# Exponential pieces in single buffers, some of them made by an accumulating DMA, with a new set of planner limits

## The chip, the cores and the metric

The kernel runs on one core of a Trainium2 chip. The metric is the device time of one execution in microseconds. The core has a tensor engine (TensorE; PE in the profile, with its weight loads as PEld), a vector engine (VectorE, DVE), a scalar engine (ScalarE, ACT), GpSimd (POOL), a sync engine that issues DMAs (SyncE, SP), and 16 DMA engines.

## The reference

Two attention blocks over one input are mixed by a gate. Only the first, the full attention, is touched by the change in its inner part.

```python
x = A_x                                            # 1 x 2048 x 512, 32 heads of 16
g = _sigmoid((x * gate_w).sum(-1, keepdims=True))
# A: full attention
scores = jnp.einsum("bhqd,bhkd->bhqk", q, k) * Dh ** -0.5
p = _softmax(scores, axis=-1)
a = (p @ v) @ wo
# B: each query sees 8 keys, at distances 0, 2, .. 14
logits = jnp.einsum("bhsd,bhswd->bhsw", q, kg) * Dh ** -0.5
b = (_softmax(masked logits) @ vg) @ wo
return g * a + (1 - g) * b
```

The 32 heads x 2048 queries x 2048 keys of A make 134 million exponentials, and they are most of the work.

## The kernel before

**Tiles.** A score tile is 128 keys by 512 queries of one head. There are 2048: 32 blocks (four column groups `ct`, four query chunks `qc`, two parities `par`), and in each 16 key tiles `kt` for four heads `j`. A tile is made by one matmul with 32 rows (L1870; four heads stand in four row groups of the array), or, for key tile 9, by four column-tiled matmuls on a spread copy of the keys (`kz`, L1855). Its exponential is multiplied with the values (`vaug`, which carries a column of ones for the denominator) by a matmul with 128 rows and 32 columns (L1643), four of them side by side in the array, one for each head.

**Two ways to an exponential.** ScalarE takes two or three tiles out of PSUM in one instruction (L1924) and writes bf16 to one of eight `pt` tiles. VectorE takes single tiles of the key tiles in `KD` (L1562): one multiply and add that ends as an int16, whose bits are read as an fp16, which is a coarse power of two. One such piece is too coarse, so the exponential is the sum of `NP_` = 3 pieces, whose bits differ by a constant, with three weights. Pieces 1 and 2 are made from piece 0 by adding a constant (`piece`: L1571 on VectorE, or L1569 on POOL, which adds pairs of int16 as one int32). The weights sit in scaled copies of the values (`vaugw`), so each such tile costs three product matmuls in place of one. Up to four tiles (`YB_ITEMS`) form a batch, whose pieces are made by one instruction of up to 128 x 2048.

**Buffers.** A batch holds one of three `yb` buffers, each with room for all three pieces (3 x 2048 int16 to a partition). It comes free when all of its product matmuls are out (`ref["refs"]` in `emit_pv_one`).

**The order.** The order on each engine is written out by a planner (`run`) when the kernel is built. It keeps a clock for each engine, always moves the one that is furthest behind, and picks its next work by due times, readiness and limits (`tune`). TensorE refills one of two PSUM slots with scores for ScalarE (three banks and two) when the slot is free; otherwise it does product matmuls, or a step of the other work (projections, the whole of attention B, output projections). `d_wanted` says whether VectorE is to take a tile too; it asks that a buffer is free and that VectorE's backlog is under a limit. `LEVELS` holds the possible values of each limit and `STRETCH` which of them holds in each of 64 equal stretches of the program. `TUNE` holds the release and due times of the other work. Each engine then runs its list in order; what it waits for are semaphores.

**POOL and VectorE.** A POOL step is made to wait for the last VectorE instruction marked `port` that stands before it (in `take_step`), and the planner does not start a marked VectorE step while POOL is busy by its clock.

**The end.** `outproj_last` handles the last two output tiles. Their two casts (L1472, one on VectorE and one on ScalarE) fill the halves of one tile, and the last of them issues one DMA for both (L1475).

Of the kernel before, what the change touches and what calls it, by code (L numbers as in the profile page):

```python
# [40 lines left out]
PW_S = tuple(s - math.log2(3.127444) for s in (0.0, -0.3330078125, 0.3330078125))  # L41
NP_ = len(PW_S)
KD = (2, 4, 7, 9, 12, 14)
KZ = (9,)
# [3 lines left out]
NPT = (4, 4)  # L48
NYB = 3
NQM = 3  # L50
# [4 lines left out]

TUNE = dict(relL=64, dueL2=2040, R0=74, R1w=42, R1g=20, R2g=31, R3g=46, R3w=50, dueB=61, dueL=84, v2rel=79, v2step=21, v2due=91, krel=230, krel2=192, ahead=0.142, dueV=30, dueS=115, dueO=678, dlast=62, qrel=28, prelB=59, prodrel=-12)

LEVELS = dict(
    pool=(0.0, 0.4, 1.2, 2.5, 4.0),
    backlog=(0.758, 1.231, 1.61, 1.894, 2.273, 2.841, 3.788),  # L60
    backlog_s=(0.888, 1.442, 1.886, 2.219, 2.663, 3.329, 4.438),
    part_us=(0.6, 0.975, 1.275, 1.5, 1.8, 2.25, 3.0),
    misc_slack=(-32, -18, -12, -8, -4, 2, 16),
    urgent=(-25, -11, -5, -1, 3, 9, 23),
    fit=(0.0, 0.2, 0.3, 0.4, 0.5, 0.6, 0.8),
    port=(0.338, 0.549, 0.718, 0.845, 1.014, 1.268, 1.69),
    alone=(-8.973, -0.273, -0.123, 0.027, 0.177, 0.327, 9.027),
    grab=(1, 0, 2, 3, 4),
    lend=(1, 0, 2, 3, 4, 5, 6, 7),
    order=((-1, 0, 1, 2, 1), (-1, 1, 0, 2, 3), (-1, 0, 2, 1, 3), (-1, 0, 1, 2, 3), (1, 0, 1, 2, 3), (0, 0, 1, 2, 3), (1, 0, 2, 1, 3), (2, 0, 1, 2, 3)),  # L70
)
STRETCH = dict(
    pool="1343344333433432333333333333232333333333333330333301233333333333",
    backlog="3333333333133333333333333333633333663333433463333133346332333333",
    backlog_s="3330413333333333333333323333033331333333631333333333331333332333",
    part_us="6333115334333333333333333533333333333643633330333335333333363303",
    misc_slack="3336333333533323333333333333333333333033333323333333433333303333",
    urgent="3341331533633333332533333333333333333333333303333333230333033331",
    fit="3613335633413353333333330333333111333333333340323333031333133333",
    port="3333533433333333333333332333333333435333333333333333333533333333",  # L80
    alone="2333333333333303333323333313333335133533303333333333333333333333",
    grab="0004204000034000030000003000000000000300000040000000300000000300",
    lend="0001000200000010000000000600000000000000000000401000006000020000",
    order="3003600020460000000144002001060007000000600020000000500060072000",
)
# [636 lines left out]
T_P1 = lambda n: n / 390.0 + 0.2  # L722
T_PI = lambda n: n / 1150.0 + 0.12
T_P2 = lambda n: n / 470.0 + 0.065
MM = 0.216
# [29 lines left out]
class _Fast:  # L755
# [15 lines left out]
    def setup(self):  # L771
# [17 lines left out]
                   for a, (w, n) in enumerate(zip(ACT_W, NPT))]  # L789
        self.yb = [c([P, NP_, YB_ITEMS * 512], I16, name=f"yb{i}") for i in range(NYB)]  # L790
        self.oT = [c([P, S], BF16, name=f"oT{i}") for i in range(2)]
# [76 lines left out]
        nc.gpsimd.memset(self.halo[:], 0.0)  # L868
        for k in range(1, NP_):
            nc.gpsimd.memset(self.pc[:, k:k + 1], round(1024.0 * (PW_S[k] - PW_S[0])) * 65537)  # L870
        self.idx = pidx, pf, ei, ef
# [587 lines left out]
    def outproj_last(self, st, i, norm):  # L1459

        nc = self.nc

        def mmh(srcs):
            for br, ct in srcs:
                o = self.oT[ct] if br == "A" else self.oB(ct)
                w = self.woA if br == "A" else self.woB
                self.mm4(self.misc, lambda c: o[:, st * 128 + 32 * c:st * 128 + 32 * c + 32], w[:, ct, :],
                         start=(br == "B" and ct == 0), stop=(br == "A" and ct == 3))

        def ev():  # L1470
            ob = self.eg[:].bitcast(BF16).rearrange("p (t n) -> p t n", t=2)
            (nc.scalar.copy if i else nc.vector.tensor_copy)(out=ob[:, i, :], in_=self.misc[:])  # L1472
            self.out_left -= 1
            if self.out_left == 0:
                nc.sync.dma_start(out=self.o_dst[:, st - i:st - i + 2, :], in_=ob)  # L1475
        order = [("B", c) for c in range(4)] + [("A", c) for c in range(4)]
        ch = self.chain([("PE", 2 * MM, lambda: mmh(order[0:2])), ("PE", 2 * MM, lambda: mmh(order[2:4])),
                         ("PE", 3 * MM, lambda: mmh(order[4:7])), ("PE", MM, lambda: mmh(order[7:])),
                         (("DVE", "ACT")[i % 2], T_D1(512), ev)],
                        due=TUNE["dueL2"] + i, rel=2048 - TUNE["relL"], deps=[self.oB_done[(st // 4, c)] for c in range(4)])  # L1480
        ch[3].deps.append(norm)
        for s in ch[:4]:
            s.hold = False

    def run(self):
        self.out_left = 2
        nc, tc = self.nc, self.tc
# [16 lines left out]
        pt_refs = {}  # L1504
        yb_free = [0.0] * NYB
        batch = None
# [52 lines left out]
        def exp_dve(slot_item):  # L1559
            (b, kt, j), bt, i, bank = slot_item  # L1560
            A = SCALE * math.log2(math.e) * 1024.0
            return nc.vector.tensor_scalar(out=self.yb[bt["buf"]][:, 0, i * 512:(i + 1) * 512], in0=bank[:],  # L1562
                                           scalar1=A, scalar2=1024.0 * (15.0 + PW_S[0]), op0=ALU.mult, op1=ALU.add)

        def piece(bt, k, gp=False):
            n = len(bt["items"]) * 512
            y = self.yb[bt["buf"]]
            if gp:
                return nc.gpsimd.tensor_tensor(out=y[:, k, 0:n].bitcast(I32), in0=y[:, 0, 0:n].bitcast(I32),  # L1569
                                               in1=self.pc[:, k:k + 1].to_broadcast([P, n // 2]), op=ALU.add)  # L1570
            return nc.vector.tensor_scalar(out=y[:, k, 0:n], in0=y[:, 0, 0:n],  # L1571
                                    scalar1=float(round(1024.0 * (PW_S[k] - PW_S[0]))), scalar2=None, op0=ALU.add)

        def close_batch():
# [3 lines left out]
            n = len(bt["items"]) * 512  # L1578
            bt["refs"] = NP_ * len(bt["items"])
            parts = [dict(n=NP_) for _ in bt["items"]]  # L1580

            def done(k, end):
                for i, it in enumerate(bt["items"]):
                    add_pv(it, self.yb[bt["buf"]][:, k, i * 512:(i + 1) * 512].bitcast(F16), end, ("y", bt, k), parts[i])
            now = min(t.values())
            pl = max(0.0, t["POOL"] - now) + sum(s.cost for s in self.steps if s.eng == "POOL" and s.rel <= p
                                                 and ready_time(s) <= now + 1.0)
            for k in range(1, NP_):
                gp = pl < tune("pool") and n >= 1024
                pl += gp * T_PI(n)  # L1590
                s = Step("POOL" if gp else "DVE", T_PI(n) if gp else T_D4(n), lambda k=k, gp=gp: piece(bt, k, gp),
                         deps=list(bt["p1"]), due=bt["due"], cls=2)
                s.on_done = lambda end, k=k: done(k, end)
                s.port = not gp
                self.steps.append(s)
            last = bt["p1"][-1]

            def after(end, prev=last.on_done):
                prev(end)
                done(0, end)  # L1600
            if last.end is None:
                last.on_done = after
            else:
                done(0, last.end)

# [8 lines left out]
        def emit_pv_one(j, now):  # L1614
# [17 lines left out]
            else:  # L1632
                ref["refs"] -= 1
                if ref["refs"] == 0:
                    yb_free[ref["buf"]] = now + 0.45
            out = self.flex[acc[b]][32 * j:32 * j + 32, :]
# [131 lines left out]
        def d_wanted(now, flex=True):  # L1768

            if p >= N - 8 or p % 64 >= TUNE["dlast"] or not any(k in KD for r in rem[p // 64] for k in r):  # L1770
                return False
            if batch is None and min(yb_free) > now:
                return False
# [36 lines left out]
        def d_add(it, bank, p1done):  # L1810
# [3 lines left out]
            if batch is None:  # L1814
                buf = min(range(NYB), key=lambda i: yb_free[i])
                batch = dict(buf=buf, items=[], p1=[], due=0.0, blk=b)
                yb_free[buf] = INF
            bt = batch
# [66 lines left out]
        while True:  # L1885
# [80 lines left out]
            else:  # L1966
# [27 lines left out]
                else:  # L1994
# [21 lines left out]
                    full = len(av) == 4  # L2016
                    part = av and (free_p <= 1 or min(yb_free) > now + 0.5 or cold(now) or now - old > tune("part_us") or (cur == NB - 1 and left[cur] <= len({(e[1], j) for j, q in enumerate(pvq) for e in q})) or p >= N)
                    pick = None
# [93 lines left out]
```

## Time and profile before

| | us |
|---|---|
| time, median of 3 runs (703.13 to 704.62) | 703.66 |
| the profiled execution: its time | 703.66 |
| its span, first to last instruction | 701.8 |
| last exponential of ScalarE ends | 692.3 |
| last DMA is issued | 696.4 |

The profile's engine shares count the time in which an engine had at least one instruction under way. TensorE's matmuls overlap, so a busy TensorE may still do more. The chain of waits gives 55% of the span to TensorE, 21% to ScalarE and 9% to VectorE. The granted clock of TensorE was 0.997 of full speed. The DMA engines are little used in the first half of the program (slices of 0 to 2 tenths after the start) and 3 to 6 tenths busy in the second, when attention B spreads its weights and values.

A line of the groups reads: source line, engine, operation, what it writes and reads, shapes, count; then busy us and mean ns of one; then the engine's idle time just before them and what ended it. A line of the DMA issues ends with the KB of one and the median us from issue to landing.

### The profile page before, as it was taken

Reading aid. Unit: us, or ns where it says so; the run is one execution under the profiler, and the core shown is the slowest. Engines: PE = TensorE matmul, PEld = TensorE weight load, DVE = VectorE, ACT = ScalarE, POOL = GpSimd, SP = SyncE. Lnnn points to the kernel's source line nnn. Section 1 sums busy time; section 2 is a strip of 40 time slices with the busy share of each in tenths; the row PEclk is TensorE's granted clock in tenths of the full one; section 3 lists DMA queues with packets and bytes.
Section 4 is the critical chain, followed back from the end, with each engine's and each line's share of the span. In section 5 each row is a group of like instructions: output and inputs, shape, how many; then the busy total and the mean of one; then the engine's idle time right before and its main releaser. Section 6 shows DMA issues by size and latency. Waiting matters only on the chain.

```text
span 701.8 us, 21325 instructions
## 1 busy us (share of the span) xinstructions
PE 679.5 (97%) x8556; PEld 218.2 (31%) x8556; DVE 651.8 (93%) x1093; ACT 680.6 (97%) x696; POOL 429.3 (61%) x364
## 2 busy tenths in 40 slices
PE   9999999999999999999998999999999999999996
PEld 4432222233322232223332223322233232222343
DVE  6999999997899999999999999999999999989982
ACT  6999999999999999999999999999999999999994
POOL 4766877766476455555456566666557564676671
PEclk9999999999999999999999999999999999999999
DMA  6001101000100100000103236356453644566521
GB/s 174 5 16 36 44 3 31 2 2 9 35 2 16 25 1 5 6 2 9 34 2 92 102 90 157 105 147 157 111 143 95 155 133 107 142 161 167 149 68 35
DMA packets 64473, 48.70 MB, mean 69 GB/s; under 512 B 22512, under 2 KB 63984, under 8 KB 64240
## 3 DMA queue, kind: packets, MB, share of 16 engines
q1 hardware_dynamic: 63808, 45.96, 25.6%
q8 instruction: 69, 1.13, 0.7%
q0 software_dynamic: 288, 1.05, 0.5%
q14 instruction: 36, 0.29, 0.1%
q10 hardware_dynamic: 272, 0.26, 0.1%
HBM read 39.85 MB, written 5.26 MB: 64 GB/s over the span
## 4 chain that ended last, share of the span: by engine, by line
PE 55%; ACT 21%; DVE 9%; issue 6%; SPq 4%; DMA 3%; POOL 1%; DVEq 0%; ACTq 0%; POOLq 0%
ACT pt L1924 21%; PE fps L1870 19%; PE fps L1643 18%; PE fps L895 14%; DVE yb L1562 5%; DVE yb L1571 2%; SPq L1328 1%; DVE prod L1229 1%; SPq L962 1%; PE fps L1855 1%; PE fps L1378 1%; DMA vw<-v_dram 1%; DMA erb<-er_dram 1%; SPq L1354 1%; DMA er<-er_dram 1%
## 5 line engine op out<-in xcount | busy, mean ns | idle before, releaser
L1924 ACT ACTIVATE pt<-fps 128x1024 bf16<-128x1024 f32 (+1 forms) x682 | 674.6, 1141 | 7.7 <-PE fps L1870 5.5
L1562 DVE TENSOR_SCALAR yb<-fps 128x512 int16<-128x512 f32 x584 | 377.0, 678 | 18.2 <-PE fps L1870 15.4
L1870 PE MATMUL fps<-qm,kT 32*128 32x512 bf16 x1976 | 285.9, 384 | 12.7 <-ACT pt L1924 7.8
L1643 PE MATMUL fps<-pt,vaug 128*32 128x512 bf16 (+1 forms) x1562 | 234.7, 372 | 0.4 <-DVE yb L1562 0.4
L1569 POOL TENSOR_TENSOR yb<-yb,pc 128x1024 int32<-128x1024 int32 (+1 forms) x104 | 188.5, 1823 | 64.5 <-DVE yb L1571 15.2
L1643 PE MATMUL fps<-yb,vaugw 128*32 128x512 f16 (+1 forms) x1228 | 174.4, 374 | 0.6 <-POOL yb L1569 0.4
L1870 PEld LDWEIGHTS <-kT 32*128 32x128 bf16 x1976 | 80.9, 91 | 272.1 <-issue 267.2
L1571 DVE TENSOR_SCALAR yb<-yb 128x2048 int16<-128x2048 int16 (+3 forms) x206 | 132.1, 666 | 0.6
L1643 PE MATMUL fps<-yb,vaug 128*32 128x512 f16 (+1 forms) x614 | 113.0, 375 | 0.0
L1360 POOL TENSOR_TENSOR er<-er,vw 128x512 bf16<-128x512 bf16 x64 | 72.8, 1158 | 49.6 <-DVE yb L1571 29.0
L895 PE MATMUL fps<-xT,ww 128*32 128x512 bf16 (+2 forms) x1296 | 99.9, 381 | 0.2
L1360 POOL TENSOR_TENSOR erb<-erb,vw 128x512 bf16<-128x512 bf16 x64 | 72.5, 1156 | 38.4 <-DVE yb L1571 23.2
L1643 PEld LDWEIGHTS <-vaug 128*32 128x32 bf16 x2176 | 64.8, 94 | 81.7 <-issue 74.9
L1643 PEld LDWEIGHTS <-vaugw 128*32 128x32 bf16 x1228 | 45.1, 94 | 41.7 <-issue 35.1
L1229 POOL TENSOR_TENSOR prod<-bq,bk 128x512 bf16<-128x512 bf16 x32 | 34.4, 1076 | 31.4 <-DVE yb L1571 17.4
L895 PEld LDWEIGHTS <-ww 128*32 128x32 bf16 x1296 | 25.9, 95 | 31.7 <-issue 24.0
L1676 POOL TENSOR_TENSOR t<-t,rc 128x512 bf16<-128x512 f32 x15 | 15.9, 1058 | 27.0 <-DVE yb L1571 13.4
L930 POOL TENSOR_SCALAR vaugw<-vaug 128x128 bf16<-128x128 bf16 (+1 forms) x24 | 20.4, 853 | 18.4 <-DVE vaug L923 10.7
L1855 PE MATMUL fps<-qm,kz 128*32 128x512 bf16 x288 | 30.8, 383 | 0.6 <-DVE yb L1562 0.4
L1229 DVE TENSOR_TENSOR prod<-bq,bk 128x2048 bf16<-128x2048 bf16 x24 | 29.9, 1268 | 0.2
L1666 DVE STREAM_TRANSPOSE t<-fps 128x512 f32<-128x512 f32 x32 | 22.6, 706 | 2.3 <-PE fps L1643 1.9
L895 PE MATMUL fps<-woB,oB 128*32 128x512 bf16 x256 | 19.9, 382 | 0.0
(117 smaller groups left out, 306.5 us busy)
## 6 DMA issues: line engine op xcount, KB each, us to landing
vw<-v_dram SPq DMA_DIRECT2D x128, 128.0 KB, 3.1
er<-er_dram SPq DMA_DIRECT2D x128, 64.0 KB, 3.0
erb<-er_dram SPq DMA_DIRECT2D x128, 64.0 KB, 2.9
v_dram<-vs SPq DMA_DIRECT2D x16, 128.0 KB, 2.6
qm<-qs SPq DMA_DIRECT2D x112, 16.0 KB, 1.8
x_in<-in_A_x_dram SPq DMA_DIRECT2D x3, 512.0 KB, 5.4
ww<-in_B_wqkv_dram SPq DMA_DIRECT2D x12, 128.0 KB, 2.8
out_dram<-ob SPq DMA_DIRECT2D x12, 128.0 KB, 2.7
```

What stands on the lines that cost most here:

```text
L895: self.nc.tensor.matmul(out=out_ps[32 * c:32 * c + 32, 0:n], lhsT=lhsT_of(c), rhs=rhs, start=start, stop=stop, tile_position=(0, 32 * c))
L930: return self.nc.gpsimd.tensor_scalar(out=self.vw4[k][:, KD.index(st), h0:h1, 0:DH], in0=self.vaug4[:, st, h0:h1, 0:DH], scalar1=PW_W[k], ...
L1229: return e.tensor_tensor(out=pr[m % 2][:, a:b], in0=bq[ct][:, a:b], in1=bk[ct][:, o + a:o + b], op=ALU.mult)
L1360: return nc.gpsimd.tensor_tensor(out=st_["erb"][m % 4][:, g, :], in0=st_["erb"][m % 4][:, g, :], in1=st_["vw"][m % 2][:, g, :], op=ALU.mult)
L1562: return nc.vector.tensor_scalar(out=self.yb[bt["buf"]][:, 0, i * 512:(i + 1) * 512], in0=bank[:], scalar1=A, scalar2=1024.0 * (15.0 + PW_ ...
L1569: return nc.gpsimd.tensor_tensor(out=y[:, k, 0:n].bitcast(I32), in0=y[:, 0, 0:n].bitcast(I32), in1=self.pc[:, k:k + 1].to_broadcast([P, n ...
L1571: return nc.vector.tensor_scalar(out=y[:, k, 0:n], in0=y[:, 0, 0:n], scalar1=float(round(1024.0 * (PW_S[k] - PW_S[0]))), scalar2=None, op0 ...
L1643: nc.tensor.matmul(out=out, lhsT=v, rhs=r, start=start, stop=stop, tile_position=(0, 32 * j))
L1666: nc.vector.transpose(out=self.t1[:, par].rearrange("p a b -> p (a b)"), in_=self.flex[acc[b]])
L1855: nc.tensor.matmul(out=dst[32 * c:32 * c + 32, :], lhsT=self.kz[:, j, KZ.index(kt), 32 * c:32 * c + 32], rhs=self.qm[(4 * ct + qc) % NQM][ ...
L1870: nc.tensor.matmul(out=dst, lhsT=self.kT[ct % 2][32 * j:32 * j + 32, kt * 128:(kt + 1) * 128], rhs=self.qm[(4 * ct + qc) % NQM][par][32 * ...
L1924: nc.scalar.activation(out=self.pt[pi[0]][pi[1]][:, 0:n * 512], in_=self.aslot[si][:, 0:n, :].rearrange("p a b -> p (a b)"), func=ACT.Exp, ...
```

## The change

- **Single buffers.** Eight slices `ys` (2048 int16 to a partition each) and one constant tile `step` replace the three `yb` buffers; the room is the same. A batch takes one slice for its first piece, and other slices only for the pieces that are made fresh. Each slice is counted down and freed on its own (`slice_dec`). `d_wanted` asks for two free slices.
- **The first piece** is now number 1, and the constants are differences from it: `STEP_OF[0]` and `STEP_OF[2]`, the second twice the first.
- **In place.** When a batch closes, its place in its block of 64 tiles (`pos`) is compared with two limits (`acc1`, `acc2`). Past both, pieces 2 and 0 are made fresh as before; past one, only piece 2; before both, neither. A piece that is not made fresh is made later in the first slice itself: once all readers of what is there are out, POOL issues a DMA that adds the `step` tile to the slice, element by element. This can happen twice, for piece 0 and then for piece 2.
- **Other limits.** `TUNE`, `LEVELS` and `STRETCH` have new values, among them `lend`, whose usual value is now 4: ScalarE's wider slot lends its third bank whenever no other bank is free. The release of the last output projections moves from 64 tiles before the end (`relL`) to 20.
- **The end.** The last two output tiles leave in two DMAs of 128 KB, the first issued by SP and the second by ScalarE, in place of one of 256 KB by SP.

```diff
+STEP_OF = {k: round(1024.0 * (PW_S[k] - PW_S[1])) for k in (0, 2)}
+assert STEP_OF[2] == 2 * STEP_OF[0]
-NYB = 3
+NSL = 8
...
-TUNE = dict(relL=64, dueL2=2040, R0=74, R1w=42, R1g=20, R2g=31, R3g=46, R3w=50, dueB=61, dueL=84, v2rel=79, v2step=21, v2due=91, krel=230, krel2=192, ahead=0.142, dueV=30, dueS=115, dueO=678, dlast=62, qrel=28, prelB=59, prodrel=-12)
+TUNE = dict(relL=20, dueL2=2040, R0=110, R1w=42, R1g=12, R2g=31, R3g=43, R3w=50, dueB=61, dueL=84, v2rel=79, v2step=21, v2due=91, krel=230, krel2=214, ahead=0.142, dueV=-9, dueS=100, dueO=665, dlast=62, qrel=32, prelB=27, prodrel=-12)
...
-        self.yb = [c([P, NP_, YB_ITEMS * 512], I16, name=f"yb{i}") for i in range(NYB)]
+        self.ys = [c([P, YB_ITEMS * 512], I16, name=f"ys{i}") for i in range(NSL)]
+        self.step = c([P, YB_ITEMS * 512], I16, name="step")
...
+        nc.gpsimd.memset(self.step[:].bitcast(I32), STEP_OF[0] * 65537)
...
-            ob = self.eg[:].bitcast(BF16).rearrange("p (t n) -> p t n", t=2)
-            (nc.scalar.copy if i else nc.vector.tensor_copy)(out=ob[:, i, :], in_=self.misc[:])
-            self.out_left -= 1
-            if self.out_left == 0:
-                nc.sync.dma_start(out=self.o_dst[:, st - i:st - i + 2, :], in_=ob)
+            if i % 2 == 0:
+                ob = self.wk.tile([P, D], BF16, name="ob", tag="ob")
+                nc.vector.tensor_copy(out=ob[:], in_=self.misc[:])
+                nc.sync.dma_start(out=self.o_dst[:, st, :], in_=ob[:])
+            else:
+                ob = self.eg[:].bitcast(BF16)[:, 512 * (i // 2):512 * (i // 2) + 512]
+                nc.scalar.copy(out=ob, in_=self.misc[:])
+                nc.scalar.dma_start(out=self.o_dst[:, st, :], in_=ob)
...
+        def slice_dec(bt, sl, at):
+            bt["cnt"][sl] -= 1
+            bt["at"] = max(bt["at"], at)
+            if bt["cnt"][sl]:
+                return
+            if sl != bt["buf"] or not bt["ip"]:
+                ys_free[sl] = bt["at"] if sl == bt["buf"] else at
+                return
+            k = bt["ip"].pop(0)
+            bt["cnt"][sl] = len(bt["items"])
+            n = len(bt["items"]) * 512
+            d0 = Step("X", 0, None)
+            d0.end = bt["at"]
+
+            def acc():
+                nonlocal acc_q
+                acc_q = max(acc_q, t["POOL"] + T_AI) + T_AQ * n / 2048
+                s.lat = acc_q + (T_AL if p < ACC_B else T_ALB) - t["POOL"] - T_AI
+                return nc.gpsimd.dma_start(out=self.ys[sl][:, 0:n], in_=self.step[:, 0:n], accum_op=ALU.add)
+            s = Step("POOL", T_AI, acc, deps=[d0], due=bt["due"], cls=2)
+            s.on_done = lambda end: bt["done"](k, sl, end)
+            self.steps.append(s)
...
+            sls = sorted((i for i in range(NSL) if ys_free[i] <= now), key=lambda i: ys_free[i])[:NP_ - 1]
+            want = (pos >= tune("acc1")) + (pos >= tune("acc2"))
+            fresh = [2, 0][:min(len(sls), want)]
+            bt["ip"] = [k for k in (0, 2) if k not in fresh]
...
-            if batch is None and min(yb_free) > now:
+            if batch is None and sum(x <= now for x in ys_free) < 2:
```

In the built program the instruction counts change so: VectorE's exponentials of single tiles from 584 to 590, its pieces from 206 to 153, POOL's pieces from 104 to 65, accumulating DMAs from none to 90, ScalarE's exponentials from 682 to 702.

## The prediction

> **What bounds the kernel now.** I read the busy shares first, then the groups by shape, then a stretch of TensorE's timeline, then the busy times by stage, the DMA issues and the last microseconds. The shares say that three engines are nearly full and POOL is not.
>
> ```profile
> PE 679.5 (97%) x8556; PEld 218.2 (31%) x8556; DVE 651.8 (93%) x1093; ACT 680.6 (97%) x696; POOL 429.3 (61%) x364
> ```
>
> So no single engine can be relieved for a large gain: ACT's own work is what the rest is fitted around. The groups by shape give the price of each kind of work (busy us, mean ns of one, then idle time before it).
>
> ```profile
> L1924 ACT ACTIVATE pt<-fps 128x1024 bf16<-128x1024 f32 x582 | 555.5, 1078 | 4.8 <-PE fps L1870 3.1 <-PE fps L1643 0.7 <-ACT pt L1924 0.2
> L1562 DVE TENSOR_SCALAR yb<-fps 128x512 int16<-128x512 f32 x584 | 377.0, 678 | 18.2 <-PE fps L1870 15.4 <-PE fps L1855 0.5 <-issue 0.2
> ...
> L1569 POOL TENSOR_TENSOR yb<-yb,pc 128x1024 int32<-128x1024 int32 x94 | 176.9, 1893 | 59.4 <-DVE yb L1571 13.9 <-DVE yb L1562 13.5 <-PE fps L1870 10.2
> ...
> L1924 ACT ACTIVATE pt<-fps 128x1536 bf16<-128x1536 f32 x100 | 150.8, 1508 | 3.0 <-PE fps L1870 2.4 <-ACT pt L1924 0.3
> L1571 DVE TENSOR_SCALAR yb<-yb 128x2048 int16<-128x2048 int16 x178 | 121.4, 704 | 0.5
> ```
>
> An ACT exponential of two tiles lasts 1078 ns and one of three 1508 ns, but back to back they start 0.904 and 1.331 us after one another, since each overlaps its forerunner by 0.17 us. The eight that are merged in the last fence below check it: 4 x 0.904 + 4 x 1.331 + 0.17 = 9.11 against 9.14.
>
> TensorE's price is in its starts, not in its busy time (matmuls overlap). The columns are start, length, instruction, count:
>
> ```profile
> 100.36 0.39 PE L1870 MATMUL fps<-qm,kT 32*128 32x512 bf16 x2
> 100.68 0.61 PE L895 MATMUL fps<-xT,ww 128*32 128x512 bf16 x8
> 101.22 0.39 PE L1870 MATMUL fps<-qm,kT 32*128 32x512 bf16 x3
> 101.55 0.62 PE L1643 MATMUL fps<-pt,vaug 128*32 128x512 bf16 x8
> 101.99 0.39 PE L1643 MATMUL fps<-yb,vaug 128*32 128x512 f16 x4
> 102.31 0.39 PE L1870 MATMUL fps<-qm,kT 32*128 32x512 bf16 x3
> ```
>
> The score matmuls (row tiles) take 0.32 us until the next column-tiled work, two passes of four column tiles take 0.54, three take 0.76. So a pass costs 0.216 us and each change of tiling 0.108 us.
>
> The stages are 128 score tiles each (16 of them, cut at the score matmul of every 128th tile). Two of them, as time, then busy of PE, PEld, DVE, ACT, POOL:
>
> ```profile
> 94.90:134.50 39.60, 39.52 (x503) 11.15 (x499) 38.19 (x64) 39.49 (x43) 28.43 (x17) 1.00 0.07 16
> ...
> 306.80:349.20 42.40, 40.70 (x422) 12.98 (x421) 42.08 (x65) 42.40 (x45) 20.01 (x19) 1.00 0.08 18
> ```
>
> The early stage is set by TensorE with ACT just behind, the middle one by ACT with VectorE just behind.
>
> **The change part by part.** The profiled execution has a span of 701.8 us and took 703.66, 1.9 of it outside the span; 703.66 is also the median, so what I add to the span I add to the median. Counts of the changed program are from its instruction order.
>
> ACT: wide exponentials fall from 100 to 55, two-tile ones rise from 582 to 646, and one of a single tile is new. 582 x 0.904 + 100 x 1.331 = 659.2 becomes 646 x 0.904 + 55 x 1.331 + 0.5 = 657.7, so -1.5 us: six tiles fewer (1464 to 1458), but more starts.
>
> TensorE: 2300 passes become 2284 (fuller groups: product groups of four column tiles go from 688 of 954 to 735 of 936), and changes of tiling rise from 1367 to 1385. -16 x 0.216 + 18 x 0.108 = -1.5 us.
>
> VectorE: six more exponentials at 0.678 (+4.1) and 53 fewer pieces (178 to 135 of the large form at 0.704, and 28 to 18 smaller ones, -34.7 by their rows): about -31 us. POOL: 104 pieces become 65 (-70.0 by 1.893, 1.465 and 1.039 us), but it issues 90 accumulating DMAs. The only POOL-issued transfers in the trace kept it 1.307 and 0.811 us, so +73 to +118 and by their mean +95. POOL goes from 429 to between 432 and 477 us of 702 and stays the emptiest; its rise costs nothing while that quarter of idle time covers it, and were it gone the pieces would be late for the product matmuls, in order on TensorE. An issue that waits there for the last reader of a slice holds back what is behind it on POOL, the products for er, erb and prod: their fold and logit matmuls come tens of us later. The new fill of the step tile is one more memset in set-up (the vaug fill of half its bytes took 1.01 us there), ahead of 7.3 us in which POOL waits for vaug, so nothing.
>
> What these sums do to the end depends on which engine sets each stage. For each stage I took the largest of ACT, TensorE and VectorE work by the prices above. Before, the 16 maxima sum to 675.2; after, to 671.6: -3.6, of which the first stage gives 1.3, the fourth 1.4, the fifth 1.4, and the third, thirteenth and fourteenth take back 1.9, 1.0 and 1.1. Cut twice as finely (32 stages), the sums are 680.1 and 680.4: +0.3. The eight ACT output tiles hold about 8 us of work, the stages are 42 and 21 us long, so neither cut is the truth; I take the middle, -1.7, and keep -3.6 and +0.3.
>
> VectorE's freed 31 us are not on the path where it only waits for scores (15.4 us of its idle time ends with L1870). They help where TensorE waits for VectorE: its groups show 2.4 us before L1870 and 0.4 each before L1643 and L1855, 3.2 in all. Bounds 0 and, if the roughly 12 us by which the 14 inner stages exceed their maxima all came from a full VectorE, -12; nearest are the 3.2, and I take -1.8, a bit over half of them.
>
> The end of the program:
>
> ```profile
> 683.11 9.14 ACT L1924 ACTIVATE pt<-fps 128x1536 bf16<-128x1536 f32 x8 [0.27 <-ACT pt L1924]
> ...
> 695.55 0.69 DVE L1472 CAST eg<-fps 128x512 bf16<-128x512 f32 x1 [0.66 <-PE fps L895]
> 695.76 0.59 ACT L1472 CAST eg<-fps 128x512 bf16<-128x512 f32 x1 [3.51 <-PE fps L895]
> 696.37 0.38 SPq L1475 DMA_DIRECT2D out_dram<-eg  x1
> ```
>
> ```profile
> out_dram<-ob SPq DMA_DIRECT2D x12, 128.0 KB, 2.7
> ...
> woB<-in_B_wo_dram POOLq DMA_DIRECT2D x1, 512.0 KB, 4.7
> wAv<-in_A_wo_dram POOLq DMA_DIRECT2D x1, 512.0 KB, 3.9
> ...
> out_dram<-eg SPq DMA_DIRECT2D x1, 256.0 KB, 3.5
> ```
>
> Two 128 KB transfers on two queues replace one of 256 KB: the last lands 2.7 to 2.8 us after its issue, not 3.5, so -0.7 or so. The bounds: 0 if the two share the engines, -0.9 if the first is already away. After the last product matmul the new order has 96 projection matmuls (24 passes) where the old has 56 (14): 2.2 us more of TensorE's tail, taken out of earlier stages; it is in the stage sums.
>
> The accumulating DMAs themselves are the unknown. The trace has no accumulation and no transfer within SBUF of this size. Nearest are the two 512 KB loads above from POOL's queue: 4.7 and 3.9 us to landing. An accumulation reads twice as much; 128 KB lands in 2.7, so 384 KB more costs 1.2 to 2.0, and a doubled read 1.6 to 2.7 on top: from 3.9 to 7.4 us. Against that stands the order: from a DMA's place to the first matmul that reads the slice there are, counted in ACT starts, 4.5 us at least, 5.4 to 6.3 for most of the 53 before the middle of the program, and 7.7 to 9.9 for most of the 37 after it. If landing takes at most 4.7, three DMAs are late by 1 us together, which I price at 0: ACT starts understate the time between by some 5%. If it takes 6.0, 33 are late by 21 us in sum; if 7.4, the sum is over 80. I take the rows as they are, and keep the rest for the range.
>
> The Trainium skill gives a fit for software-queue DMAs ("DMA: Bandwidth & Descriptors", Anatomy of one DMA): about 2.0 us plus the bytes at 436 GB/s. That would make 3.2 us of 512 KB and 4.4 of twice that, both early enough; the rows are 0.7 to 1.5 slower than the fit, and the rows stand.
>
> One rule speaks against the change. In the trace POOL's operations wait for VectorE's pieces (13.9 us before L1569). The Trainium skill ("SBUF — State Buffer", SBUF: two separate sides, with its example in the part on the bandwidth-pool intuition) says that a DMA from GpSimd's queue cannot get its descriptors written while VectorE runs in a two-port mode, and shows 620 ns becoming 3100. Were each of the 90 delayed by one such piece at 0.7 us, landing would go from 4.3 to 5.0 and the six tightest would be late by 2 us together; were each delayed by the 2.5 of that example, landing would be 6.8 and the lateness some 55 us. No run here shows either yet.
>
> The sum: -1.7 (stages) - 1.8 (VectorE's relief) - 0.7 (end) + 0 (DMAs) = -4.2: 703.66 - 4.2 = 699.5.
>
> **The rivals.** *Accumulations land late* (slower). Place: TensorE, in order, stands before the first product matmul that reads an accumulated slice, and the scores for ACT queue up behind it. Half of the lateness is taken up where ACT sets the stage, so landing after 6.0 costs 21 / 2 = 10.5 us: 699.5 + 10.5 = 710.0. Break-even is near a landing of 5.5 (7 us in sum, 3.5 net). For it: the double read, and 24 of the early gaps are below 5.5. Against: both rows of this size are below 5. Chance 0.24.
>
> *Balance is no better than before* (no change). The fine cut says +0.3, VectorE's relief is nothing because it was never last, and only the end is left: 703.66 + 0.3 - 0.7 = 703.3. For it: ACT and TensorE lose only 1.5 us each, and of 308 pieces 218 are made as before, so the DMA does little of what the change is named for. Against: the coarse cut, and the 3.2 us. Chance 0.18.
>
> *VectorE was the hidden limit.* The stage maxima fall by 3.6 and half of the 12 us of excess goes: -3.6 - 6 - 0.7 = -10.3: 693.4. For it: in stages six, eight, ten and thirteen VectorE's work is within 0.5 us of the largest before, in the new order only in the seventh. Against: only 3.2 us of TensorE's idle time ends with it. Chance 0.16.
>
> **How the numbers follow.** The forecast, 699.5 with its own range 696 to 702.2, has 0.42. The time of this kernel is told from no change at about 0.2%, 1.4 us. Faster by more: 0.42 + 0.16 = 0.58. Within it: 0.17 of the balance rival. Slower: late landings 0.24 and 0.01 of the rest, 0.25. Late landings beyond 709 have about 0.11 and gains below 693 about 0.08, so the range is 693 to 709.
>
> **What would show it.** Right: accumulations to landing at 5 us or below; no product matmul of L1690 with more than 2 us of idle in sum that a DMA ends; VectorE busy near 620; the two last outputs landing in 2.7. Wrong: a landing of 6 us or more, TensorE idle before L1690 ended by the accumulations, or ACT's start-to-start excess grown, above all in stages one to eight, where the gaps are shortest. The prediction is also wrong if POOL's idle is gone and its products hold up the fold matmuls.

## The result, and the profile after

| | before | after |
|---|---|---|
| time, median of 4 runs (lowest to highest), us | 703.39 (703.05 to 704.62) | 756.28 (754.23 to 761.15) |
| ratio, 95% interval | | 1.0759 (1.0699 to 1.0818) |
| the profiled execution: time / span, us | 703.66 / 701.8 | 761.15 / 759.3 |
| granted clock of TensorE, mean | 0.997 | 0.965 |

The kernel became 7.6% slower, about 53 us. The page of the changed kernel first: busy shares, the granted clock in 40 slices, the chain of waits, then groups and DMA issues, with the columns as before (line numbers moved: L1870 is now L1917, L1924 is L1971, L1571 is L1584, L1643 is L1690, L1562 is L1575, L895 is L905).

```profile
PE 706.2 (93%) x8531; PEld 219.9 (29%) x8531; DVE 642.2 (85%) x1046; ACT 686.9 (90%) x716; POOL 443.5 (58%) x416
...
PEclk9999999999999998999999999999989999898899
...
PE 43%; DMA 23%; ACT 13%; DVE 9%; issue 4%; POOL 3%; SPq 3%; ACTq 0%; POOLq 0%; DVEq 0%
...
L1971 ACT ACTIVATE pt<-fps 128x1024 bf16<-128x1024 f32 (+1 forms) x702 | 680.7, 1097 | 55.9 <-PE fps L1917 52.0
...
L1604 POOL DMA_DIRECT2D ys<-step x90 | 80.9, 954 | 55.8 <-PE fps L1917 31.7
...
L1690 PE MATMUL fps<-ys,vaug 128*32 128x512 f16 (+1 forms) x620 | 86.2, 387 | 22.6 <-DMA ys<-step 20.9
...
ys<-step POOLq DMA_DIRECT2D x86, 512.0 KB, 5.7
vw<-v_dram SPq DMA_DIRECT2D x128, 128.0 KB, 3.8
...
v_dram<-vs SPq DMA_DIRECT2D x16, 128.0 KB, 4.0
```

The instruction counts are those that were forecast, so no engine got more work than was counted. ACT's busy time is 6 us up, but its idle time before an exponential went from 7.8 (4.8 and 3.0 in its two large forms) to 55.9 us. DMA, 3% of the chain of waits before, now holds 23% of it. The 86 accumulations of full size (L1604) land after a median of 5.7 us, and transfers beside them got slower too: `v_dram<-vs` 4.0 us where it was 2.6, `vw<-v_dram` 3.8 where it was 3.1. Who waits for them is in the view of the waits (total us, times, longest):

```profile
ACT pt L1971 <- PE fps L1917: 52.0, 64, 3.0
...
PE fps L1690 <- DMA ys<-step: 21.4, 21, 2.7
...
DVE vs L1345 <- DMA v_dram<-vs: 14.9, 7, 6.0
```

TensorE waits 21.4 us for accumulations, ACT 52.0 us for scores. The first is less than half of what was lost, so the link between them has to be looked at in a stretch of time. Here GpSimd issues four accumulations within five microseconds (start, length, then the instruction):

```profile
271.26 1.75 POOL L1604 DMA_DIRECT2D ys<-step  x2 [1.96 <-PE fps L1690]
273.88 0.85 POOL L1604 DMA_DIRECT2D ys<-step  x1 [0.87 <-DVE ys L1584]
...
275.43 1.19 POOL L1604 DMA_DIRECT2D ys<-step  x1
```

and this is TensorE's timeline a little later:

```profile
278.53 0.40 PE L1690 MATMUL fps<-ys,vaugw 128*32 128x512 f16 x4 [0.53 <-DMA ys<-step]
...
281.22 0.40 PE L1690 MATMUL fps<-ys,vaug 128*32 128x512 f16 x4 [0.55 <-DMA ys<-step]
...
285.18 0.62 PE L1690 MATMUL fps<-ys,vaug 128*32 128x512 f16 x4 [2.70 <-DMA ys<-step]
...
287.59 0.61 PE L1917 MATMUL fps<-qm,kT 32*128 32x512 bf16 x3
288.13 0.62 PE L1690 MATMUL fps<-pt,vaug 128*32 128x512 bf16 x4
...
291.11 0.39 PE L1917 MATMUL fps<-qm,kT 32*128 32x512 bf16 x2
291.43 0.62 PE L905 MATMUL fps<-xT,ww 128*32 128x512 bf16 x8
```

The first of the four had landed at 275.8, 4.6 us after its issue. The other three land at 278.5, 281.2 and 285.1, that is 2.7, 2.7 and 4.0 us behind one another, and TensorE stands at each. After the last wait the same score pass takes 0.54 us to the next work (287.59 to 288.13) where it takes 0.32 a little later (291.11 to 291.43): here the granted clock in the profile is 0.5, from 283.5 to 290.3. I call such a stretch a half-clock window. The sums by stretch show it (us; busy of PE, PEld, DVE, ACT, POOL; clock; DMA share; GB/s):

```profile
275.00:282.00 7.00, 5.89 (x66) 1.73 (x63) 6.23 (x9) 6.49 (x8) 2.57 (x4) 1.00 1.07 201
282.00:292.00 10.00, 7.27 (x94) 1.93 (x93) 5.88 (x12) 6.24 (x7) 4.94 (x5) 0.66 0.46 88
```

Inside the program the trace of before has one such half-clock window, of 3.4 us; this one has ten, of 51 us together, each 3.4 us or a multiple.

### The profile page after: what moved, and what is told of

Its sections match the earlier page's. It is cut to its first block, busy times and chain, and to the rows that moved or that the text cites. A ratio compares the mean times of both kernels' runs of the same rounds, so it can differ in the third digit from the quotient of the medians.

```text
span 759.3 us, 21354 instructions
## 1 busy us (share of the span) xinstructions
PE 706.2 (93%) x8531; PEld 219.9 (29%) x8531; DVE 642.2 (85%) x1046; ACT 686.9 (90%) x716; POOL 443.5 (58%) x416
## 3 DMA queue, kind: packets, MB, share of 16 engines
q0 software_dynamic: 13248, 47.19, 32.6%
## 4 chain that ended last, share of the span: by engine, by line
PE 43%; DMA 23%; ACT 13%; DVE 9%; issue 4%; POOL 3%; SPq 3%; ACTq 0%; POOLq 0%; DVEq 0%
PE fps L1917 15%; PE fps L1690 14%; DMA ys<-step 13%; ACT pt L1971 13%; PE fps L905 11%; DVE ys L1575 4%; DMA vw<-v_dram 4%; DMA v_dram<-vs 3%; DMA erb<-er_dram 2%; DVE ys L1584 2%; DMA er<-er_dram 2%; SPq L1364 1%; SPq L1338 1%; POOL ys L1604 1%; PE fps L1388 1%
## 5 line engine op out<-in xcount | busy, mean ns | idle before, releaser
L1971 ACT ACTIVATE pt<-fps 128x1024 bf16<-128x1024 f32 (+1 forms) x702 | 680.7, 1097 | 55.9 <-PE fps L1917 52.0
L1575 DVE TENSOR_SCALAR ys<-fps 128x512 int16<-128x512 f32 x590 | 381.6, 680 | 50.4 <-PE fps L1917 45.6
L1917 PE MATMUL fps<-qm,kT 32*128 32x512 bf16 x1987 | 298.8, 392 | 17.4 <-ACT pt L1971 5.2
L1690 PE MATMUL fps<-pt,vaug 128*32 128x512 bf16 (+1 forms) x1556 | 228.6, 381 | 0.3 <-DVE ys L1575 0.2
L1690 PE MATMUL fps<-ys,vaugw 128*32 128x512 f16 (+1 forms) x1240 | 192.1, 381 | 2.6 <-DVE ys L1584 1.4
L1582 POOL TENSOR_TENSOR ys<-ys,pc 128x1024 int32<-128x1024 int32 (+1 forms) x65 | 123.3, 1898 | 75.8 <-DVE ys L1575 22.9
L1917 PEld LDWEIGHTS <-kT 32*128 32x128 bf16 x1987 | 81.5, 91 | 288.7 <-issue 284.5
L1604 POOL DMA_DIRECT2D ys<-step x90 | 80.9, 954 | 55.8 <-PE fps L1917 31.7
L1584 DVE TENSOR_SCALAR ys<-ys 128x2048 int16<-128x2048 int16 (+3 forms) x153 | 108.2, 729 | 1.5
L1690 PE MATMUL fps<-ys,vaug 128*32 128x512 f16 (+1 forms) x620 | 86.2, 387 | 22.6 <-DMA ys<-step 20.9
L1690 PEld LDWEIGHTS <-vaug 128*32 128x32 bf16 x2176 | 69.0, 95 | 115.7 <-issue 109.9
L905 PE MATMUL fps<-xT,ww 128*32 128x512 bf16 (+2 forms) x1296 | 100.0, 384 | 0.5 <-DVE ys L1575 0.4
L1370 POOL TENSOR_TENSOR erb<-erb,vw 128x512 bf16<-128x512 bf16 x64 | 75.2, 1235 | 40.4 <-DVE ys L1584 18.4
L1690 PEld LDWEIGHTS <-vaugw 128*32 128x32 bf16 x1240 | 48.6, 95 | 46.7 <-issue 41.3
L905 PEld LDWEIGHTS <-ww 128*32 128x32 bf16 x1296 | 25.8, 95 | 33.1 <-issue 26.3
L940 POOL TENSOR_SCALAR vaugw<-vaug 128x128 bf16<-128x128 bf16 (+1 forms) x24 | 20.6, 859 | 19.3 <-DVE vaug L933 10.1
L1713 DVE STREAM_TRANSPOSE t<-fps 128x512 f32<-128x512 f32 x32 | 22.5, 704 | 10.9 <-PE fps L1690 10.8
L1345 DVE CAST vs<-fps 128x512 bf16<-128x512 f32 x16 | 11.0, 686 | 17.1 <-DMA v_dram<-vs 14.9
```

The costliest lines, as they stand in the source:

```text
L905: self.nc.tensor.matmul(out=out_ps[32 * c:32 * c + 32, 0:n], lhsT=lhsT_of(c), rhs=rhs, start=start, stop=stop, tile_position=(0, 32 * c))
L1370: return nc.gpsimd.tensor_tensor(out=st_["erb"][m % 4][:, g, :], in0=st_["erb"][m % 4][:, g, :], in1=st_["vw"][m % 2][:, g, :], op=ALU.mult)
L1575: return nc.vector.tensor_scalar(out=self.ys[bt["buf"]][:, i * 512:(i + 1) * 512], in0=bank[:], scalar1=A, scalar2=1024.0 * (15.0 + PW_S[1 ...
L1582: return nc.gpsimd.tensor_tensor(out=dst.bitcast(I32), in0=src.bitcast(I32), in1=self.pc[:, k:k + 1].to_broadcast([P, n // 2]), op=ALU.add)
L1584: return nc.vector.tensor_scalar(out=dst, in0=src, scalar1=float(STEP_OF[k]), scalar2=None, op0=ALU.add)
L1604: return nc.gpsimd.dma_start(out=self.ys[sl][:, 0:n], in_=self.step[:, 0:n], accum_op=ALU.add)
```

## The experiments

All but two start from the changed kernel and keep its order on every engine. Most edit only the line in `acc` that issues an accumulation; where that is replaced by a small write, pieces 0 and 2 of those batches are not made, so that the exponentials there are coarser, while the matmuls that read them run as before. Times are medians; the ratio is to the kernel before, run on the same chip (704 to 705 us there; 703.39 for the change itself). "Landing" is the time from a DMA's issue until its data are there.

### What an accumulation costs: left out, a quarter of it, a copy, other elements

```diff
-return nc.gpsimd.dma_start(out=self.ys[sl][:, 0:n], in_=self.step[:, 0:n], accum_op=ALU.add)
+# e1_left_out
+return nc.gpsimd.memset(self.ys[sl][:, 0:n].rearrange("p (a b) -> p a b", b=512)[:, :, 0:2], 0.0)
+# e2_quarter
+return nc.gpsimd.dma_start(out=self.ys[sl][0:32, 0:n], in_=self.step[0:32, 0:n], accum_op=ALU.add)
+# e3_copy
+return nc.gpsimd.dma_start(out=self.ys[sl][:, 0:n], in_=self.step[:, 0:n])
+# e4_int32
+return nc.gpsimd.dma_start(out=self.ys[sl][:, 0:n].bitcast(I32), in_=self.step[:, 0:n].bitcast(I32), accum_op=ALU.add)
```

> The order of the changed kernel on every engine, but the 90 accumulations are left out: in the place of each DMA, POOL writes two columns of each item of the slice (so the pieces that they would make are wrong). Theory (late landings stall TensorE, and each stall costs clock besides): no transfer, no lateness, so 697 to 706 us, and half-clock windows inside the program at 0 to 2 in place of 10. Rival (the new limits and the order are themselves worse, the DMAs only show it): 735 us or more.

> The same order, each accumulation covers 32 of 128 partitions (the rest of each piece is left out): a quarter of the bytes from the same queue. If bytes and the queue of one behind the other make the lateness: landing near 3 to 3.5 us in place of 5.7, and 698 to 710 us. If a fixed price of POOL's queue makes it (descriptors, VectorE's hold on the port): landing over 4.5 and more than 735 us.

> The same order and bytes to each slice, but a plain copy of the step tile in place of the accumulation (the added pieces are wrong). If the second read of the accumulation is the price: landing 3.9 to 4.3 us when nothing else runs, and 705 to 722 us. If a 512 KB transfer is as slow without the add: landing 4.5 at least and 745 us or more.

> The same order, each accumulation adds pairs as 32-bit words: half the elements, the same bytes. If the adder is paid by the element: 1 us between landings of DMAs in a row in place of 2.0 to 2.6, and 700 to 720 us. If by the byte: landing and time as in the changed kernel, 750 to 762.

| run | us | ratio (95%) | landing us: least / median / most |
|---|---|---|---|
| e1_left_out | 706.56 | 1.0036 (1.0019 to 1.0053) | none |
| e2_quarter (128 KB each) | 707.46 | 1.0053 (1.0035 to 1.0071) | median 3.45 |
| e3_copy (512 KB, no add) | 726.21 | 1.0318 (1.0281 to 1.0354) | 2.84 / 3.74 / 11.9 |
| e4_int32 (half as many elements) | 756.49 | 1.0723 (1.0674 to 1.0772) | 4.49 / 5.67 / 14.8 |
| the change itself | 756.28 | 1.0759 (1.0699 to 1.0818) | 4.49 / 5.70 / 15.2 |

The time of e1_left_out is half a us above the range I had given it, and far below its rival's. The rest of the change, with its order, limits, slices and end, costs 2.3 us (706.56 against 704.22); the accumulations cost 756.28 - 706.56 = 49.7 (by the ratios, each to its own chip, 50.9). It is not GpSimd's time for issuing them: in e2_quarter GpSimd is busy for 434.0 us, against 443.5 in the change and 368.1 in e1_left_out, and that run is 0.9 us behind e1_left_out. The page and waits of e1_left_out show what is gone with them:

```profile
PE 683.9 (97%) x8531; PEld 218.0 (31%) x8531; DVE 630.0 (89%) x1046; ACT 679.5 (96%) x716; POOL 368.1 (52%) x416
```

```profile
ACT pt L1971 <- PE fps L1917: 9.1, 14, 2.1
ACT eg L1487 <- PE fps L905: 5.7, 1, 5.7
```

TensorE's busy time is 22 us less for the same 8531 matmuls: at half clock each lasts longer. An add is paid by its bytes, not its elements (e4 equals the change), and needs 1.65 us more than a copy of the same bytes (4.49 against 2.84). The copies still cost 19.7 us, between the two ranges that I had given, and little of it is waiting for the copies themselves. TensorE's waits in e3_copy:

```profile
PE fps L1690 <- DMA ys<-step: 2.0, 3, 1.1
```

The profiled span is 18.4 us longer than in e1_left_out. By the stages of 128 score tiles, the last eight are 20.2 us longer, the first eight 1.8 shorter. Copies hurt where attention B's transfers run, then, and not by being waited for.

### Where they cost: the early half, the late half, and the early ones that stand alone

```diff
+# e5_early: e1's small write instead, where p >= ACC_B (tile 1100)
+# e6_late:  e1's small write instead, where p < ACC_B
+# e12_spaced
+at, lastacc[0] = acc_q - lastacc[0], acc_q
+if p >= ACC_B or at < 5.0:
+    return nc.gpsimd.memset(self.ys[sl][:, 0:n].rearrange("p (a b) -> p a b", b=512)[:, :, 0:2], 0.0)
 return nc.gpsimd.dma_start(out=self.ys[sl][:, 0:n], in_=self.step[:, 0:n], accum_op=ALU.add)
```

> The order of the changed kernel, accumulations kept only before tile 1100 (about 53 of 90), the later ones left out as in the run without any. Theory (one behind another they land late; in the first half little else is on the DMA engines, so lateness comes from their own queueing at 2 to 2.6 us each): stages 1, 2, 3 and 7 stay as long as in the changed kernel, stages 11 to 16 as in the run without accumulations: 722 to 732 us. Rival (the loss is traffic against attention B's loads): 706 to 712.

> The complement: accumulations kept only from tile 1100 on (about 37). Theory: these meet the loads of attention B, land at 6 to 12 us and delay those loads too (v_dram, vw, erb), which the plan did not allow for: 728 to 740 us. If the early ones are the whole loss: 706 to 712.

> The order of the changed kernel with 25 of its 90 accumulating DMAs: those of the first half that the order puts at least 5 us behind the one before. The other 65 are left out (a small write to the tile in their place), so the output lacks these parts. Theory (an accumulation costs by its queue: alone it lands in 4.5 to 6.0 us, as in the mixed run, and TensorE waits for such ones under 2 us in sum): 706.6 of the order without any accumulation plus 2 to 3, so 708 to 711, and no window at half clock beyond that run's. Rival (every accumulation is late or slows what lies beside it, alone as in a row): 25 of 48 early ones share the 13.1 us of the early half by number, 6.8, or more, so 713 or more.

e5_early took 719.65 us (1.0243, 1.0182 to 1.0303; its four runs went from 717.9 to 726.7), e6_late 741.25 (1.0523, 1.0498 to 1.0548): 13.1 and 34.7 over e1_left_out, together 47.8 of the 49.7, so the halves add up. Both lie just outside the ranges I had given for the theory (722 to 732 and 728 to 740), and far from those of the rivals. e12_spaced took 708.66 (1.0052, 1.0033 to 1.0071): 25 accumulations that stand alone cost 2.1 us over e1_left_out by the medians and 1.1 by the ratios, whose intervals overlap. (Of the 512 KB ones the early half has 54 and not 48, so its rival's share by number is 6.1, 712.7; the run stays 4 below.) Its tile view and its waits (L1694 is L1690 there):

```profile
DMA to landing us min/median/max: 4.5/5.0/6.1
```

```profile
PE fps L1694 <- DMA ys<-step: 1.5, 4, 0.9
```

The same DMA, with the same order around it, makes TensorE wait 1.5 us in sum, in four places, when it is alone. In the late half, the waits of e6_late show a second way by which time goes:

```profile
DVE vs L1345 <- DMA v_dram<-vs: 12.6, 5, 5.1
...
PE fps L1690 <- DMA ys<-step: 7.4, 8, 1.7
...
PE fps L1917 <- DVE vs L1345: 6.0, 2, 3.7
```

VectorE cannot overwrite `vs` before attention B's store of it has left. That store is late beside the accumulations, VectorE stands for it, and TensorE then waits for VectorE. In e1_left_out nothing of this is among TensorE's waits.

From these profiles I made an account by stage (the 16 stretches of 128 score tiles): the stage's length less that in e1_left_out, beside half of the added half-clock time (a halved clock is taken to lose half of it), TensorE's waits for accumulations, and its waits for `vs`, each over all lines, with waits that are too short for the views. Sums over the stages, us:

| run | longer than e1_left_out | half clock / 2 | waits for the DMAs | waits for `vs` | correlation over stages |
|---|---|---|---|---|---|
| the change | 53.7 | 23.7 | 21.7 | 5.8 | 0.91 |
| e5_early | 10.4 | 1.7 | 9.8 | 0.0 | 0.99 |
| e6_late | 32.2 | 16.8 | 7.4 | 6.0 | 0.99 |
| e3_copy | 18.4 | 10.8 | 2.1 | 2.6 | 0.98 |

The three terms give 51.2 of 53.7, and another split comes out close: in the change TensorE is busy 22.3 us longer than in e1_left_out with the same matmuls, and idle 31.4 us longer. By single stages the account is rougher. The seventh stage has 7.7 us by the three terms and is 5.3 longer, since its window lies partly over a wait; the fourteenth has 2.0 and is 4.8 longer. So the division is an estimate. In e5_early six of the first nine stages have waits of 0.6 to 0.9 us in sum and are 0.9 to 1.0 longer, at full clock: there a wait of TensorE is paid one for one.

### Filling the waits

If TensorE had work while it waits, would the clock stay up? Before the 18 longest waits, matmuls with zero weights were put in, 419 in all; they add nothing to the sums.

```diff
+for _ in range(self.fill_n):
+    for j in js0:
+        nc.tensor.matmul(out=self.flex[acc[cur]][32 * j:32 * j + 32, :], lhsT=self.wz[:, 0:32],
+                         rhs=self.wz[:].unsqueeze(1).to_broadcast([P, 4, P]), start=False, stop=False, tile_position=(0, 32 * j))
```

> The changed kernel, all accumulations in place, with idle matmuls of zeros (added to running sums, so that nothing changes in the result) in front of the 18 product matmuls that waited longest, as many as fill the wait that was measured there. The waits stay, but TensorE is not idle in them. If half of the loss is the halved clock after each wait: half-clock windows fall from 10 to 3 or fewer, and 728 to 742 us. If the clock is a bystander and the waits are the loss: 752 to 765 us.

768.29 us (1.0883, 1.0849 to 1.0916): a miss, above both ranges. The waits for accumulations fell to 9.3 us, but TensorE's idle time in all fell only from 53.1 to 43.9 us while its busy time rose by 21.2, and six half-clock windows, 41 us together, were still inside the program, at other places. So this run does not part the share of the clock from that of the waits; the account and TensorE's busy time above are the only evidence for the 23.7.

### The adds on GpSimd instead, and a mixture

```diff
+# e9_pool: all 90; e11_mix: all but the 25 of e12_spaced, which stay DMAs
+return nc.gpsimd.tensor_tensor(out=self.ys[sl][:, 0:n].bitcast(I32), in0=self.ys[sl][:, 0:n].bitcast(I32), in1=self.pc[:, 0:1].to_broadcast([P, n // 2]), op=ALU.add)
```

> The order of the changed kernel, and all 90 pieces are made in place, but by an addition on POOL (1.9 us, pairs as 32-bit words) where the DMA was issued. Theory (what costs is the landing and the traffic, not the working in place): done 2 to 3 us after its start, no transfers, so near the run without any: 705 to 713 us, half-clock windows 0 to 2. Rival (POOL's queue is the next limit: 90 us more of work on it, which the plan knows nothing of, hold up the products and collide with VectorE's pieces): 718 us or more.

> The order of the changed kernel; an accumulation stays a DMA only before tile 1100 and where the plan has at least 5 us between it and the last (25 of 90), the other 65 are made by POOL in place. Theory (a DMA by itself lands in 4.5 to 4.9 us, which the plan allows for; what is late is the second one of a row, and all of them beside attention B's loads): within 3 us of the run with POOL alone, no half-clock window inside after the first 40 us. Rival (POOL-issued DMAs are late even alone): 8 us or more above that run.

e9_pool took 756.4 us (1.0744, 1.0718 to 1.077), e11_mix 744.77 (1.0569, 1.0549 to 1.059). The groups by shape and the waits of e9_pool:

```profile
L1604 POOL TENSOR_TENSOR ys<-ys,pc 128x1024 int32<-128x1024 int32 x86 | 163.5, 1908 | 32.5 <-PE fps L1690 12.0 <-DVE prod L1239 7.7 <-DVE ys L1584 5.7
...
L1584 DVE TENSOR_SCALAR ys<-ys 128x2048 int16<-128x2048 int16 x135 | 120.2, 911 | 1.4
```

```profile
PE fps L1690 <- DVE ys L1584: 13.5, 21, 1.6
...
PE fps L1690 <- POOL ys L1582: 5.9, 10, 1.1
```

An add on GpSimd lasts 1.9 us, less than any landing, and yet the time is the same: GpSimd rises to 530 us busy, its operations meet VectorE's pieces, which last 911 ns in place of 698 in e1_left_out, and now those are late. Half-clock windows came too, without any accumulating DMA: 40 us of them where e1_left_out has 5. My expectation of 705 to 713 missed; the time and the waits are as the rival had it. In e11_mix the 25 lone DMAs land in a median of 4.93 us and TensorE waits under 2 us for them; since those 25 without the GpSimd adds make 708.66 (e12_spaced), the rest of its loss comes with the 65 adds. I had expected a time within 3 us of e9_pool's and no half-clock window after the first 40 us; it is 11.6 us below that time and has five such windows, so this missed too.

### The limits without accumulations, and the end alone

e8_fresh makes all pieces fresh (nine slices, no `step` tile) and is planned anew with the change's limits; e10_two_out is the kernel before with only the change's two output DMAs.

```diff
+# e8_fresh, against the change
-NSL = 8
+NSL = 9
-            want = (pos >= tune("acc1")) + (pos >= tune("acc2"))
+            want = 2
-            if batch is None and sum(x <= now for x in ys_free) < 2:
+            if batch is None and sum(x <= now for x in ys_free) < 3:
+# e10_two_out, against the kernel before
-            if self.out_left == 0:
-                nc.sync.dma_start(out=self.o_dst[:, st - i:st - i + 2, :], in_=ob)
+                nc.sync.dma_start(out=self.o_dst[:, st, :], in_=ob[:])
...
+                nc.scalar.dma_start(out=self.o_dst[:, st, :], in_=ob)
```

> Single buffers and the new limits, but planned anew without any accumulation: every piece fresh, nine slices (the step tile's room is the ninth). If single buffers and the limits are worth something by themselves: 696 to 703. If the limits only fit a plan with accumulations, or single buffers bring nothing: 704 to 716. VectorE gets its pieces back (some 650 us busy).

> The kernel before, with only its last two output tiles leaving in two DMAs, one from SP and one from ACT. The prediction's term: -0.7 us, so 703.0 to 704.2 where the kernel before has 704.4 on this chip. Rival: two queues at once gain nothing, 704 to 705.

e8_fresh: 727.27 us (1.0311, 1.029 to 1.0331), with a mean clock of 0.997 and no large wait: its work is more (VectorE 653.2 us busy, ACT 693.5). Both of my ranges (696 to 703, 704 to 716) missed. The limits were found for another plan, so this run says little on the change; it only shows that they bring no gain in a plan without accumulations. e10_two_out: 704.64 against 704.91, ratio 0.9997 (0.9987 to 1.0008). Its last output DMA is on ACT's queue:

```profile
out_dram<-eg ACTq DMA_DIRECT2D x1, 128.0 KB, 3.6
```

128 KB of two transfers issued 0.1 us apart land after 3.4 and 3.6 us, the 256 KB before after 3.5: the split gains nothing.

## Why the prediction was wrong

**The failed step** is the price of the accumulating DMAs: landing at most 4.7 us, "which I price at 0". It had three faults.

- *One landing time for all.* The two rows it was taken from, 4.7 and 3.9, are loads at the start of the program. Alone and early, an accumulation lands in 4.49 to 6.14, median 5.05 (e12_spaced): the bounds 3.9 to 7.4 held it, the value taken was too low. What no bound held is the queue. Before 370 us, 24 of 49 accumulations were issued before the one ahead had landed, and those landings lie 2.47 to 5.88 us apart, median 2.84 (the planner books `T_AQ` = 1.8 for each). After 370 us they share the DMA engines with attention B's transfers: median 6.4, a tenth above 10.1, the last 15.2. A median row can't stand for this; the tail and the rows of several do the harm.
- *Absorption.* The rival "Accumulations land late" had 21 us of lateness at a landing of 6.0 and took half as absorbed, 10.5. The sum was nearly right, by luck: it meant 33 accumulations each late by a little, and 21.4 us came from 21 waits of up to 2.7. Nothing was absorbed: e5_early is 10.4 us longer for 9.8 us of waits. TensorE, busy for 96% of that run's span, is full as well, and while it waits it makes no scores for ACT.
- *Two costs without a term*: the halved clock behind the waits, 23.7 by the account, and attention B's own transfers made late, 5.8. So the rival's place and mechanism were right, and its 710.0 was 46 short.

**The other terms**, read from e1_left_out. *Stages, -1.7*: its 14 inner stages took 590.7 against 592.0, -1.3, so near. Single stages moved as the maxima had said: the third +2.4 (forecast +1.9), the fourth and fifth -1.4 each (-1.4 each), the thirteenth and fourteenth +1.3 and +1.0 (+1.0 and +1.1). But the first stage, from which 1.3 less had been forecast, is 3.4 longer (1.7 of it a half-clock window that e2_quarter's profile does not have; there it is 1.5) and the last 1.7: ACT waits 5.7 us for the last projections where it waited 3.5, and these 2.2, which I had put into the stage sums as taken out of earlier stages, stay at the end. *VectorE's relief, -1.8*: VectorE's busy time did fall, by 22 us to 630.0, and TensorE's waits for its exponentials and pieces fell from 3.2 to 1.2 us (one of 2.1 for `vaug` is new, in the first stage), but the inner stages hold no gain beyond the -1.3. It was nothing, as the rival "Balance is no better" had it. *The end, -0.7*: nothing (e10_two_out); its bound 0 was right. Together -4.2 became +2.3, a small error beside the DMAs'.

**What held**: the counts, GpSimd's busy time (443.5, forecast 432 to 477), GpSimd's issues (954 ns, between the 811 and 1307 taken), and as signs to look for, TensorE's idle time before L1690 and ACT's excess. The landing, 5.70 in the median, fell between its two marks of 5 and 6. VectorE was busy for 642.2 us, not near 620, and the last two outputs landed in 3.5 and 3.0 us, not in 2.7. One sign was in the wrong place: I looked for the loss in stages one to eight, where the gaps are shortest; against e1_left_out they are 15.5 us longer, the other eight 38.2. The gaps there are longer, but the landings and what runs beside them grew more.

**Two terms taken from pages.** The Trainium skill's fit ("DMA: Bandwidth & Descriptors", Anatomy of one DMA), with the bytes doubled, made 4.4 us: that is close to the least landing, 4.49, and says nothing of the second in a row. The lock-out ("SBUF — State Buffer", SBUF: two separate sides) did not show: in e5_early, of the early ones without another in front, those with a piece of VectorE in the 2.5 us behind the issue landed in a median of 4.70 (7 of them), those without in 4.99 (15).

**Open.** How the late half's loss of 34.7 us divides between waiting for the accumulations and their traffic beside attention B's was not parted. e3_copy comes near: with as many bytes written, and 2.0 us of waits for its copies in the whole program, its last eight stages are 20.2 us longer, so traffic alone can cost much there. A copy keeps the DMA engines busy for less time than an add, though (the packets of GpSimd's queue took 18.1% of the engines' span, against 32.6% in the change). The share of the clock is an estimate.

## What to carry to other kernels

Price a DMA that an in-order engine waits for by its landing when two or three are in its queue and when the rest of the program's transfers run, not by a lone one: here the lone ones (25 in e12_spaced) cost about 2 us and all 90 cost 50. On a TensorE that was nearly full no wait was absorbed, and short waits cost about as much again through the clock, by the estimate above. Work moved off an engine that the others hardly wait for (22 us of VectorE here) bought nothing.

## What was not expected of the hardware

- A 512 KB add inside SBUF from GpSimd's queue lands in 4.49 us at best, a copy in 2.84; int16 and int32 take the same time (5.70 and 5.67 in the median); adds of this size in a row land at least 2.47 us apart in the change, some 210 GB/s of destination.
- Half-clock windows came without a long wait: the longest of TensorE's waits in the change is 2.70 us, and a 3.4 us window begins at or just behind single waits of 2.1 (68 us into the program), 2.0 (497) and 1.8 us (640). The Trainium skill ("TensorE: Matmul & The Clock Gate", Why this matters for your kernels) warns of gaps of more than about 3 us; the trace shows that shorter ones can do it. What counts seems to be the sum in a slice of time. All windows of a run start and end on one grid of 3.41 us. In the 14 profiles (start and end of the program left out), each of the 32 full-clock slices of its grid in which TensorE was idle for 1.45 us or more is followed by one at half clock, and none of the 2637 with under 0.5 us is; between the two, 19 of 168 are. In e12_spaced, where no wait for a DMA is longer than 0.9 us, the only window inside the program is the one that e1_left_out has too. No run varied this by itself.
- In e9_pool VectorE's large pieces take 683 ns (median) beside an idle GpSimd; the 60 or so that met a GpSimd operation took a median of some 990 ns and up to 2.4 us.
